# One stream of 2368 score slots in place of 1184 turns of two scores, with B's maxima packed in full banks and spread beside the next unit

## The chip, the core and the metric

The kernel runs on one core of a Trainium2 chip. Its five engines work side by side and meet by semaphores: TensorE (PE in the profile, its weight loads PEld), VectorE (DVE), ScalarE (ACT), GpSimd (POOL) and SyncE (SP), which issues most DMAs. Each engine takes its instructions in order. Matmul results land in PSUM, eight banks of 512 fp32 columns on 128 partitions, and have to be read from there by VectorE or ScalarE. The metric is the device time of one execution in microseconds (us).

## The reference

Two attention layers run over the same 2048 x 512 input with 32 heads of 16 dimensions. Their outputs are mixed by a gate per token.

```
A: p = softmax(q k^T / 4) over all 2048 keys; o = p v; a = o @ wo
B: four segments of 512 tokens; in each
   p = softmax(q k^T / 4 + causal mask) over the segment's own keys; a_dot = p v
   a_mem = phi(q) M / (phi(q) z + 1e-6)          phi(t) = t + 1 if t > 0, else exp(t)
   o = g * a_mem + (1 - g) * a_dot               g = sigmoid(beta), by head
   M += phi(k)^T v;  z += sum of phi(k)
   b = o @ wo
out = s * a + (1 - s) * b                        s = sigmoid(x . gate_w)
```

## The kernel before

**First stage.** The projections of both sides are made chunk by chunk of 512 tokens (`CH`), each as three products of a high and a low part (L312), and put in DRAM, q and k with both halves, v with a column of ones. B's memory is built on the way. Some maxima are computed here already (`some_max`).

**Main stage.** The work is cut in units: a side (A or B), a group `g` of four heads (eight groups) and a chunk `c` of 512 queries (four). That makes 32 units of A and 32 of B, one of each after the other.
In a unit of A, the scores of a block of 128 keys against the 512 queries are one matmul for each head, 128 keys on the partitions, 512 columns (st, L626). A head's q and k, cut in parts, take 50 rows, so heads 0 and 1 lie in the lower 64 partitions and heads 2 and 3 in the upper 64 (`rows`): two products on different halves can run at the same time. ScalarE takes the exponential of a bank (L638) into `p`. Value products (ops, L674) multiply `p` by v and the ones for the four heads side by side, 17 columns of weights each, and add up over all keys in one PSUM bank `ops`. At the end of a unit ScalarE copies `ops` (L678) and SP stores it (L679).

**Maxima.** The softmax subtracts each row's maximum before the exponential. For that, the scores are computed a second time the other way round, 128 queries on the partitions and 512 keys in the columns (sm, L180), and VectorE reduces each bank (L197). This runs `LEAD` turns ahead of the scores. When a unit's maxima are there, `finish_max` reduces them once more and negates them (L159), POOL splits them into a high and a low part (L163, L164), PE transposes them (L170), ScalarE copies them (L172), and two DMAs, issued on ScalarE's queue (L174), write them as two more rows of the q tile, rows 48 and 49. The unit's first score needs these rows.
For B, of the 4 x 4 blocks of 128 queries by 128 keys only the lower triangle counts. Before, a unit's maxima are five turns of two banks. The first two turns take query block 3 against all 512 keys with a mask added (L209). In the others a bank holds 256 columns that VectorE reduces straight (L217, L223) and 256 columns on the diagonal that ScalarE copies to `dg` (L216, L222), POOL masks (L225) and VectorE reduces `MASK_T` turns later.

**Order.** All is written by hand (`manual_schedule`); the loop over turns at the end of `gated_mix` sets it. A turn is two scores and two maxima, alternating, then the value products of the turn `LAG` = 4 before, then transposes (`run_late`), reduces that were put off (`after_max`), and output products. Everything else hangs on turn numbers: `beside` (loads, factors, scaling) and `fill` (output products, six at a time, four such runs for 128 rows of the output). A unit of A has 32 turns (8 x 4 head pairs by key blocks), one of B five. Heads 0 and 1 are scored in even turns while the maxima take 2 and 3; odd turns the other way round.
PSUM in the main stage: three banks for maxima (`sm_ps`), three for scores (`st_ps`), one for `ops`, one for output products and transposes (`ms_ps`).

**End of the pipeline.** When a chunk's units are done, the sums of the softmax are inverted (`recip`, `invert`), the outputs are scaled (POOL), split in two parts, and multiplied by both `wo` (`out_products`, 24 matmuls for 128 rows, L762). The last chunk is done in pieces (`piece`).

Of the kernel before, what the change touches and what calls it, by code (L numbers as in the profile page):

```python
# [19 lines left out]
D = 512  # L20
# [12 lines left out]
TURNS = {"A": 32, "B": 5}  # L33
LEAD = 44
LAG = 4
LATE_T = 6
MASK_T = 4
PRE = 10
NK = 10
# [3 lines left out]
def gated_mix(ctx, tc, x, xT, wqkv, a_wo, b_wq, b_wk, b_wv, b_wo, beta, gate_w, out):  # L43
# [8 lines left out]
    for side in "AB":  # L52
        for o in range(NO):
            for c in range(NCH):
# [17 lines left out]
    cmask = const.tile([128, CH], F32, name="cmask")  # L72
    nc.gpsimd.memset(cmask, 0.0)
    nc.gpsimd.affine_select(out=cmask, in_=cmask, pattern=[[-1, CH]], base=384, channel_multiplier=1,
                            compare_op=ALU.is_ge, fill=MASKED)
# [18 lines left out]
    sm_ps = ctx.enter_context(tc.tile_pool(name="sm_ps", bufs=3, space=PSUM))  # L94


    units = []
    for c in range(NCH):
        for g in range(NG):
            pair = [("A", g, c), ("B", g, c)]  # L100
            units += pair if c < NCH - 1 else pair[::-1]
    units.insert(1, units.pop(2))
    turns = [(u, j) for u in units for j in range(TURNS[u[0]])]
    first = {}
    for t, (u, j) in enumerate(turns):
        if j == 0:
            first[u] = t
    end = {u: first[u] + TURNS[u[0]] for u in units}
    seg_end = {(s, c): max(end[s, g, c] for g in range(NG)) for s in "AB" for c in range(NCH)}

# [7 lines left out]

    kbuf = [kp.tile([128, 2, CH], F32R, name=f"k{i}") for i in range(NK)]
    knext = [0]  # L120
# [11 lines left out]
    def load_k(u, kc):  # L132

        side, g, c = u
        t = kbuf[knext[0] % NK]
        knext[0] += 1
# [12 lines left out]
    pmt = {}  # L149
    late = []  # L150
    masked = []

    pmB = [mp.tile([128, 4, 4, 2], F32, name=f"pmB{i}", bufs=1) for i in range(2)]
# [3 lines left out]
    def finish_max(u):  # L157
        nm = mp.tile([128, 4, 4], F32, tag="nm", name="nm")
        nc.vector.tensor_reduce(nm, pmt.pop(u), axis=AX.X, op=ALU.max, negate=True)  # L159
# [7 lines left out]
    def transpose_max(u, ms, pool, tag):  # L167
# [5 lines left out]
        for r in range(2):  # L173
            nc.scalar.dma_start(raw(qt[u])[64 * r + 48:64 * r + 50], raw(mt)[16 * r:16 * r + 16])  # L174
# [4 lines left out]
    def max_product(ps, u, h, s, n0, n, k):  # L179
        nc.tensor.matmul(ps[:, n0:n0 + n], rows(qt[u][:, :, s * 128:(s + 1) * 128], h, 48), rows(k[:, :, :n], h, 48),  # L180
                         start=True, stop=True)

    def max_parts(m):

        u, j = turns[m]
        side, g, c = u
        if j == 0:
            pmt[u] = (mp.tile([128, 4, 4, 4], F32, tag="pmA", name="pm") if side == "A" else pmB[(c * NG + g) % 2])
        pm = pmt[u]
        heads = (2, 3) if m % 2 == 0 else (0, 1)  # L190

        def part_a(e):

            ps = sm_ps.tile([128, CH], F32, tag="sm", name="sm")
            h, s, kc = heads[e], j // 2 % 4, j // 8
            max_product(ps, u, h, s, 0, CH, kt_[u, kc])
            nc.vector.tensor_reduce(pm[:, h, s, kc:kc + 1], ps, axis=AX.X, op=ALU.max)  # L197

        dg = dp.tile([128, 4, 128], F32, tag="dg", name="dg") if side == "B" and j > 1 else None

        def part_b(e):
            k = kt_[u, c]
            ps = sm_ps.tile([128, CH], F32, tag="sm", name="sm")
            if j < 2:
                h = heads[e]
                max_product(ps, u, h, 3, 0, CH, k)
                nc.vector.tensor_tensor_reduce(ps, ps, cmask, 1.0, -3.0e38, ALU.add, ALU.max, pm[:, h, 3, 0:1])  # L209
                return  # L210
            two = dg[:, 2 * e:2 * e + 2]
            if j < 4:
                h = heads[e]
                max_product(ps, u, h, 0, 0, 128, k)
                max_product(ps, u, h, 2, 128, 384, k)
                nc.scalar.copy(two, blocked(ps)[:, 0::3])  # L216
                nc.vector.tensor_reduce(pm[:, h, 2, 0:1], ps[:, 128:384], axis=AX.X, op=ALU.max)  # L217
            else:
                h = heads[0] if e == 0 else 2 - heads[0]
                for f in range(2):  # L220
                    max_product(ps, u, h + f, 1, 256 * f, 256, k)
                nc.scalar.copy(two, blocked(ps)[:, 1::2])  # L222
                nc.vector.tensor_reduce(pm[:, h:h + 2, 1, 0], blocked(ps)[:, 0::2], axis=AX.X, op=ALU.max)  # L223
            if e == 1:
                nc.gpsimd.affine_select(out=dg, in_=dg, pattern=[[0, 4], [-1, 128]], base=0, channel_multiplier=1,  # L225
                                        compare_op=ALU.is_ge, fill=MASKED)
                h0 = heads[0]

                def reduce():
                    if j < 4:  # L230
                        out, src = pm[:, h0:h0 + 2, 0::2, 1], dg.rearrange("p (h s) t -> p h s t", h=2)
                        nc.vector.tensor_reduce(out, src, axis=AX.X, op=ALU.max)  # L232
                    else:
                        for h, two in ((h0, dg[:, 0:2]), (2 - h0, dg[:, 2:4])):
                            nc.vector.tensor_reduce(pm[:, h:h + 2, 1, 1], two, axis=AX.X, op=ALU.max)  # L235
# [751 lines left out]
```

## Time and profile before

| | |
|---|---|
| Three runs | 2124.81, 2143.61, 2156.91 us (median 2143.61) |
| The profiled execution's own time | 2130.38 us |
| Its span, first to last instruction | 2128.7 us |
| Mean granted clock of TensorE | 0.966 |
| PE busy | 2033.5 us (96%), 16705 matmuls |
| PEld busy | 950.7 us (45%) |
| DVE busy | 1645.0 us (77%) |
| ACT busy | 1510.5 us (71%) |
| POOL busy | 315.1 us (15%) |
| 345 to 2105 us alone | PE 1698.6, DVE 1456.9, ACT 1384.8, POOL 293.8 of 1760; clock 0.97, DMA share 0.35 |

How to read it: busy time is a union, so an engine whose instructions overlap by their tails counts each moment once. A matmul's row begins when it is issued and its end is modelled; PE counts as busy whenever a row is open, at half the clock too. So PE's 96% says that PE is rarely without a row, not that it streams all the time.

The costliest groups of the page, with the mean time of one in ns and the idle time before them:

```profile
L197 DVE TENSOR_REDUCE pm<-sm 128x1 f32<-128x512 f32 x2048 | 1270.7, 683 | 162.3 <-PE sm L180 133.5
L638 ACT ACTIVATE p<-st 128x512 f32<-128x512 f32 x2048 | 1134.7, 604 | 310.1 <-PE sm L180 163.2
L180 PE MATMUL sm<-k,qA 48*128 48x512 f32 x2048 | 804.0, 467 | 10.5 <-DVE pm L197 8.3
L626 PE MATMUL st<-qA,k 50*128 50x512 f32 x2048 | 772.7, 455 | 20.6 <-ACT p L638 19.3
L674 PE MATMUL ops<-p,vA 128*17 128x256 f32 x8192 | 659.8, 395 | 12.6 <-ACT oraw L678 12.5
```

Each value product of the program stands twice in the trace, as two passes.

### The profile page before, as it was taken

The numbers are of one execution on the slowest core, as the hardware profiler recorded it, in microseconds if no ns is written. First come the engines' busy times: TensorE is split into PE (matmuls) and PEld (weight loads), VectorE is DVE, ScalarE is ACT, GpSimd is POOL, SyncE is SP. The second block draws the span as 40 slices with busy tenths as digits, with TensorE's granted clock in tenths as the row PEclk, the third lists the DMA queues.
The fourth block names the chain that finished last, engine by engine and source line by source line (L and its number), as shares of the span: only waits on it lengthen the run. The fifth ranks groups of instructions, "written<-read, shape, count | busy, mean of one in ns | idle before, by whom it ended". The sixth has DMA issues, their size and how long they took to land.

```text
span 2128.7 us, 43282 instructions
## 1 busy us (share of the span) xinstructions
PE 2033.5 (96%) x16705; PEld 950.7 (45%) x16705; DVE 1645.0 (77%) x2996; ACT 1510.5 (71%) x2945; POOL 315.1 (15%) x512
## 2 busy tenths in 40 slices
PE   7999999999999999999999999999999999999996
PEld 6887664343333333444443333444433434343343
DVE  3235896899988988788889998878889998877810
ACT  3234335788887877787778887778788887776773
POOL 3000001132100102111100032111011231101130
PEclk9999998999999999899999998999999999998998
DMA  6667545545522235332222362222232642322311
GB/s 199 222 212 252 174 150 171 144 107 146 145 77 77 77 100 137 77 82 74 70 67 78 93 164 79 73 77 63 81 84 81 162 102 73 82 80 70 104 52 36
DMA packets 113629, 233.81 MB, mean 110 GB/s; under 512 B 23840, under 2 KB 38208, under 8 KB 111760
## 3 DMA queue, kind: packets, MB, share of 16 engines
q1 hardware_dynamic: 109600, 228.48, 37.9%
q8 instruction: 133, 2.18, 0.4%
q10 hardware_dynamic: 2592, 1.57, 0.3%
q0 software_dynamic: 1232, 0.99, 0.2%
q14 instruction: 72, 0.59, 0.1%
HBM read 159.07 MB, written 70.66 MB: 108 GB/s over the span
## 4 chain that ended last, share of the span: by engine, by line
PE 80%; DVE 10%; ACT 6%; DMA 2%; issue 2%; ACTq 1%; SPq 0%; DVEq 0%
PE st L626 31%; PE ops L674 27%; PE pr L312 11%; DVE pm L197 6%; PE sm L180 4%; PE fin L762 4%; ACT p L638 3%; PE fin L893 1%; DVE pmB L232 1%; DVE pmB L235 1%; ACT oraw L678 1%; ACT dg L216 1%; ACTq L174 1%; PE num L468 1%; PE mt_ps L170 0%
## 5 line engine op out<-in xcount | busy, mean ns | idle before, releaser
L197 DVE TENSOR_REDUCE pm<-sm 128x1 f32<-128x512 f32 x2048 | 1270.7, 683 | 162.3 <-PE sm L180 133.5
L638 ACT ACTIVATE p<-st 128x512 f32<-128x512 f32 x2048 | 1134.7, 604 | 310.1 <-PE sm L180 163.2
L180 PE MATMUL sm<-k,qA 48*128 48x512 f32 x2048 | 804.0, 467 | 10.5 <-DVE pm L197 8.3
L626 PE MATMUL st<-qA,k 50*128 50x512 f32 x2048 | 772.7, 455 | 20.6 <-ACT p L638 19.3
L674 PE MATMUL ops<-p,vA 128*17 128x256 f32 x8192 | 659.8, 395 | 12.6 <-ACT oraw L678 12.5
L626 PEld LDWEIGHTS st<-qA,k 50*128 50x128 f32 x2048 | 311.9, 189 | 464.4 <-ACT p L638 379.9
L180 PEld LDWEIGHTS sm<-k,qA 48*128 48x128 f32 x2048 | 325.5, 189 | 45.9 <-DVE pm L197 26.3
L674 PEld LDWEIGHTS ops<-p,vA 128*17 128x17 f32 x8192 | 136.9, 96 | 346.8 <-issue 318.0
L163 POOL CAST ms<-nm 128x16 fp32r<-128x16 f32 x64 | 12.7, 199 | 1038.6 <-DVE nm L159 1038.5
L645 ACT ACTIVATE p<-st 128x512 f32<-128x512 f32 x256 | 141.2, 604 | 22.0 <-PE sm L180 13.0
L626 PE MATMUL st<-qB,k 50*128 50x384 f32 (+3 forms) x512 | 133.5, 364 | 18.7 <-ACT p L638 17.2
L180 PE MATMUL sm<-k,qB 48*128 48x128 f32 (+3 forms) x512 | 144.7, 368 | 1.3 <-DVE pmB L217 1.2
L626 PEld LDWEIGHTS st<-qB,k 50*128 50x128 f32 x512 | 77.5, 195 | 99.7 <-ACT p L645 51.5
L360 DVE TENSOR_TENSOR q<-pr,q 128x512 fp32r<-128x512 f32 x64 | 44.0, 687 | 96.3 <-ACT q L353 90.0
L353 ACT CAST q<-pr 128x512 fp32r<-128x512 f32 x64 | 37.5, 586 | 95.8 <-PE pr L312 68.2
L674 PE MATMUL ops<-p,vB 128*17 128x256 f32 (+1 forms) x1536 | 103.7, 358 | 0.0
L630 POOL TENSOR_SCALAR_AFFINE_SELECT p<-p 128x512 f32<-128x512 f32 x128 | 79.6, 635 | 162.2 <-ACT p L645 137.3
L217 DVE TENSOR_REDUCE pmB<-sm 128x1 f32<-128x256 f32 x128 | 54.4, 425 | 53.1 <-ACT dg L216 52.9
L180 PEld LDWEIGHTS sm<-k,qB 48*128 48x128 f32 x512 | 77.9, 184 | 20.7 <-DVE pmB L217 15.8
L209 DVE CUSTOM_DVE_ANT_0 sm<-sm,cmask 128x512 f32<-128x512 f32 x128 | 84.4, 718 | 2.5 <-PE sm L180 2.5
L225 POOL TENSOR_SCALAR_AFFINE_SELECT dg<-dg 128x512 f32<-128x512 f32 x96 | 60.9, 635 | 157.4 <-ACT dg L216 133.5
L312 PE MATMUL pr<-xh,wql 128*128 128x512 f32 x128 | 55.1, 430 | 6.1 <-ACT xh L404 6.1
(171 smaller groups left out, 1667.8 us busy)
## 6 DMA issues: line engine op xcount, KB each, us to landing
k<-kdA SPq DMA_DIRECT2D x256, 128.0 KB
vA<-vdA SPq DMA_DIRECT2D x32, 544.0 KB
k<-kdA SPq DMA_DIRECT2D x256, 64.0 KB
qdA<-q SPq DMA_DIRECT2D x32, 256.0 KB
kdA<-q SPq DMA_DIRECT2D x32, 256.0 KB
qdB<-q SPq DMA_DIRECT2D x32, 256.0 KB
qA<-qdA SPq DMA_DIRECT2D x64, 128.0 KB
kdB<-q SPq DMA_DIRECT2D x32, 256.0 KB
```

The lines of the kernel that those rows point to most:

```text
L180: nc.tensor.matmul(ps[:, n0:n0 + n], rows(qt[u][:, :, s * 128:(s + 1) * 128], h, 48), rows(k[:, :, :n], h, 48), start=True, stop=True)
L197: nc.vector.tensor_reduce(pm[:, h, s, kc:kc + 1], ps, axis=AX.X, op=ALU.max)
L209: nc.vector.tensor_tensor_reduce(ps, ps, cmask, 1.0, -3.0e38, ALU.add, ALU.max, pm[:, h, 3, 0:1])
L217: nc.vector.tensor_reduce(pm[:, h, 2, 0:1], ps[:, 128:384], axis=AX.X, op=ALU.max)
L225: nc.gpsimd.affine_select(out=dg, in_=dg, pattern=[[0, 4], [-1, 128]], base=0, channel_multiplier=1, compare_op=ALU.is_ge, fill=MASKED)
L312: nc.tensor.matmul(ps, l(a, k), r(b, k), start=(n == 0), stop=(n == 11))
L626: nc.tensor.matmul(ps[:, n0:n0 + CH - q0], rows(k[:, :, b * 128:(b + 1) * 128], h, 50), rows(q[:, :, q0:], h, 50), start=True, stop=True)
L630: nc.gpsimd.affine_select(out=x, in_=x, pattern=[[0, 4], [1, 128]], base=0, channel_multiplier=-1, compare_op=ALU.is_ge, fill=0.0)
L638: nc.scalar.activation(p[:, h], ps, AF.Exp, scale=SCALE)
L645: nc.scalar.activation(p[:, h], ps, AF.Exp, scale=SCALE)
L674: nc.tensor.matmul(ops[32 * h:32 * h + 17, q0:q0 + w], v[n][:, 17 * h:17 * h + 17], p[:, h, c0:c0 + w], start=(j == 0), stop=(j == TURNS[s ...
L762: nc.tensor.matmul(ps, l[:, o], r[:, o], start=(n == 0), stop=(n == 23))
```

## The change

The main stage's turn of two scores becomes a slot of one: one score bank and one bank of maxima, 64 slots for a unit of A and ten for one of B, 2368 in all. The maxima have a list of their own (`maxs`), as long as the slots and 96 slots ahead. In it B's ten banks stand seven places apart among the maxima of the next unit of A. B's banks are packed full: in each row half two of diagonal blocks alone (four 128 x 128 products, copied to `dg` and masked as before), two with one block of query block 1 and three of query block 3, and one with query block 2 of two heads. The mask that was added (`cmask`) goes.
Heads are scored in the order 0, 2, 1, 3, so that score and maximum swap row halves at each slot.
Values wait until a block of keys has all its four heads, and go after each third slot (`BURST`), as wide as the queue allows: 512 columns for A. Output products run in three runs of eight in place of a burst of values, each run in a score bank, copied out and added by POOL. Transposes take score banks too. `sm_ps` has four banks, `ms_ps` is gone. The maxima's rows of q are written by DMAs on SP's queue instead of ScalarE's. A has eight k buffers and B two, where ten were shared. Numbers of turns become numbers of slots throughout, and some loads and stores of 1 MB are cut in four.

```diff
-TURNS = {"A": 32, "B": 5}
-LEAD = 44
-LAG = 4
-LATE_T = 6
-MASK_T = 4
-PRE = 10
-NK = 10
+SLOTS = {"A": 64, "B": 10}
+NU = 32
+LEAD = 96
+BURST = 3
+RUN = 8
+GAP = {"A": 3, "B": 5}
+MASK_T = 8
+LATE_T = 8
+PRE = 20
+NKA, NKB = 8, 2
...
+    maxs = []
+    for k in range(NU):
+        mine = {u: iter(range(32)) for u in range(2)}
+        bs = [k - 1] if 0 < k < NU - 1 else [k - 1, k] if k else []
+        start, apart = (34, 3) if k == 1 else (6, 7) if k < NU - 1 else (24, 3)
+        theirs = {r: [(unit("B", b), (r, i)) for b in bs for i in range(5)] for r in range(2)}
+        for p in range(64 + 10 * len(bs)):
+            r = (len(maxs) + 1) % 2
+            i = (p - start) // apart
+            if (p - start) % apart == 0 and 0 <= i < 10 * len(bs):
+                maxs.append(theirs[r].pop(0))
+            else:
+                maxs.append((unit("A", k), (r, next(mine[r]))))
...
-            nc.scalar.dma_start(raw(qt[u])[64 * r + 48:64 * r + 50], raw(mt)[16 * r:16 * r + 16])
+            nc.sync.dma_start(raw(qt[u])[64 * r + 48:64 * r + 50], raw(mt)[16 * r:16 * r + 16])
...
+            if i < 2:
+                for n in range(4):
+                    b = i + 2 * (n % 2)
+                    max_product(ps, u, h0 + n // 2, b, 128 * n, 128, k, 128 * b)
+                dg = dp.tile([128, 4, 128], F32, tag="dg", name="dg")
+                nc.scalar.copy(dg, blocked(ps))
...
+                todo.append((m + MASK_T, lambda: nc.vector.tensor_reduce(
+                    to, dg.rearrange("p (h s) t -> p h s t", h=2), axis=AX.X, op=ALU.max)))
+            elif i < 4:
+                h = h0 + i - 2
+                max_product(ps, u, h, 1, 0, 128, k)
+                max_product(ps, u, h, 3, 128, 384, k)
+                nc.vector.tensor_reduce(pm[:, 1, h, 3:7], blocked(ps), axis=AX.X, op=ALU.max)
+            else:
+                for f in range(2):
+                    max_product(ps, u, h0 + f, 2, 256 * f, 256, k)
...
+        if m == last_max[u]:
+            def finish():
+                late.append((m + MASK_T + 2 + LATE_T, u, finish_max(u)))
+            todo.append((m + (MASK_T + 1 if side == "B" else 0), finish))
...
-    ms_ps = ctx.enter_context(tc.tile_pool(name="ms_ps", bufs=1, space=PSUM, reuse_waits="tile"))
+    sm_ps = ctx.enter_context(tc.tile_pool(name="sm_ps", bufs=4, space=PSUM, reuse_waits="tile"))
...
+        h = (0, 2, 1, 3)[j % 4]
...
+            queue.extend((n + GAP[side], u, i) for i in range(j // 4 * 4, j + 1))
...
+            for h in range(4):
+                nc.tensor.matmul(ops[32 * h:32 * h + 17, q0:q0 + 128 * w], v[:, 17 * h:17 * h + 17], p[:, h, c0:c0 + 128 * w],
+                                 start=(i == 0), stop=done, tile_position=(0, 32 * h))
...
+    def out_products(c, b, i):
+
+        ps = st_ps.tile([128, D], F32, tag="st", name="fin")
+        for n in range(RUN * i, RUN * i + RUN):
...
+        t = fr.tile([128, D], F32, tag="res" if i == 0 else "more", name="res", bufs=2 if i == 0 else 1)
+        nc.scalar.copy(t, ps)
...
+        nc.gpsimd.tensor_add(t0, t0, t)
...
+    while n < nS or queue or waiting or beside or fill:
+        for f in beside.pop(n, []):
             f()
+        waiting += fill.pop(n, [])
+        if n < nS:
+            score_part(n)
+        m = n + LEAD
+        if m < nS:
             loads(m + PRE)
+            max_part(m, sm_ps)
+        run_todo(m)
+        if n % BURST == BURST - 1 or n >= nS:
+
+            filled[0] = bool(waiting) and not filled[0] and m < nS
+            if not filled[0]:
+                some_values(n)
+
+                run_late(st_ps, "st", m + 1)
+            if waiting and (filled[0] or m >= nS):
+                waiting.pop(0)()
+        n += 1
```

More of the change, by code (lines that the diff above doesn't have):

```diff
@@ L149, in gated_mix @@
     pmt = {}
+    todo = []
     late = []
-    masked = []
-    pmB = [mp.tile([128, 4, 4, 2], F32, name=f"pmB{i}", bufs=1) for i in range(2)]
+    pmB = [mp.tile([128, 2, 4, 8], F32, name=f"pmB{i}", bufs=1) for i in range(2)]
     for t in pmB:
@@ L196, in part_a @@
             max_product(ps, u, h, s, 0, CH, kt_[u, kc])
             nc.vector.tensor_reduce(pm[:, h, s, kc:kc + 1], ps, axis=AX.X, op=ALU.max)
-        dg = dp.tile([128, 4, 128], F32, tag="dg", name="dg") if side == "B" and j > 1 else None
-        def part_b(e):
+        else:
             k = kt_[u, c]
[L205 to L224, printed above, removed]
@@ L229, in reduce @@
[L229 to L235, printed above, removed]
-                masked.append((m + MASK_T, reduce))
@@ L609, in gated_mix, with score_part, score @@
     pt_ = {}
[L611 to L613 removed]
+    queue = []
+    def score_part(n):
+        u, j = slots[n]
         side, g, c = u
         q = qt[u]
[L616 to L625 removed]
+        if j % 4 == 0:
+            pt_[u, j // 4] = pp.tile([128, 4, CH], F32, tag="p", name="p")
+        p = pt_[u, j // 4]
+        h = (0, 2, 1, 3)[j % 4]
+        def score(ps, h, b, k, n0, q0):
             nc.tensor.matmul(ps[:, n0:n0 + CH - q0], rows(k[:, :, b * 128:(b + 1) * 128], h, 50),
@@ L832, in gated_mix @@
     c = NCH - 1
-    nT = len(turns)
     fins = {}
```

381 lines of the change are left out of this document (168 added, 213 removed).

## The prediction

> **What bounds the kernel now.** I read the clock first (mean 0.966), then the chain of waits, whose shares by engine are
>
> ```profile
> PE 80%; DVE 10%; ACT 6%; DMA 2%; issue 2%; ACTq 1%; SPq 0%; DVEq 0%
> ```
>
> so PE mostly. Next the timeline of one undisturbed A turn, because a share is a mean over unlike parts:
>
> ```profile
> 1002.00 0.50 PE L626 MATMUL st<-qA,k 50*128 50x512 f32 x1
> 1002.00 0.50 PE L180 MATMUL sm<-k,qA 48*128 48x512 f32 x1
> 1002.33 0.39 PE L626 MATMUL st<-qA,k 50*128 50x512 f32 x1
> 1002.34 0.39 PE L180 MATMUL sm<-k,qA 48*128 48x512 f32 x1
> 1002.66 0.63 PE L674 MATMUL ops<-p,vA 128*17 128x256 f32 x8
> 1003.22 0.50 PE L626 MATMUL st<-qA,k 50*128 50x512 f32 x1
> ```
>
> A score (st) and a maximum (sm) start together: they use opposite halves of the array's rows. From pair to pair 0.33 us, then eight value products, and 0.88 us from the second pair to the next turn's first: 1.22 us a turn. Near 2072 us, where no maxima are left, turns still come 1.22 apart (value rows at 2072.07, 2073.28, 2074.50), so this is PE's own pace and not VectorE's. The other two engines, where work is queued for them:
>
> ```profile
> 1040.86 3.67 DVE L197 TENSOR_REDUCE pm<-sm 128x1 f32<-128x512 f32 x6
> ```
>
> ```profile
> 343.87 3.54 ACT L638 ACTIVATE p<-st 128x512 f32<-128x512 f32 x7
> ```
>
> One lasts 0.68 and 0.60 us, so one follows another after (3.67-0.68)/5 = 0.598 us on VectorE and (3.54-0.60)/6 = 0.49 on ScalarE. A turn needs 1.20 of VectorE and 0.98 of ScalarE: VectorE is just under PE.
>
> Then the stops between turns. B's maxima, cut into 256 columns:
>
> ```profile
> 1029.48 0.42 DVE L217 TENSOR_REDUCE pmB<-sm 128x1 f32<-128x256 f32 x1 [0.34 <-ACT dg L216]
> 1030.24 0.42 DVE L217 TENSOR_REDUCE pmB<-sm 128x1 f32<-128x256 f32 x1 [0.34 <-ACT dg L216]
> ```
>
> VectorE and ScalarE take turns on one bank, 0.77 us a reduce. Six output products:
>
> ```profile
> 1008.09 0.73 PE L762 MATMUL fin<-wolA,hA 128*128 128x512 f32 x2
> 1008.66 1.09 PE L762 MATMUL fin<-wohA,hA 128*128 128x512 f32 x4
> 1009.68 0.49 PE L626 MATMUL st<-qA,k 50*128 50x512 f32 x1
> ```
>
> 0.23 us each in the run of four; VectorE's next reduce, at 1010.25, follows 1.51 us of idleness. The maxima's way back into q, issued on ScalarE's queue, and the clock around it (busy time of PE, its loads, VectorE, ScalarE and POOL; then clock and DMA):
>
> ```profile
> 609.34 1.28 ACTq L174 DMA_DIRECT2D qB<-mt  x2
> 610.66 1.09 ACT L638 ACTIVATE p<-st 128x512 f32<-128x512 f32 x2 [1.36 <-PE sm L180]
> ```
>
> ```profile
> 608.90:612.40 3.50, 2.36 (x21) 0.93 (x24) 2.88 (x5) 2.14 (x6) 0.00 (x0) 1.00 0.02 5
> 612.40:619.20 6.80, 6.80 (x44) 1.96 (x38) 3.64 (x7) 3.91 (x8) 0.00 (x0) 0.50 0.77 207
> ```
>
> ScalarE issues for 1.28 us and computes nothing, PE's score at 611.31 waits 0.68 us for it, and after a window with PE 67% busy the clock (0.50) is halved for 6.8 us. Value rows start 2.13 us apart there instead of 1.22: 2.9 us lost.
>
> **The sum before.** First score at 340.4, last copy of ops at 2105, span 2128.7. Between copies (L678) an A unit without output products takes 42.5 us and a B unit 7.9: 32 x 50.4 = 1613. Forty-eight stops of 1.5: 72. The stage's mean clock, 0.97, is about 110 us at half speed, 43% of it lost: 48. That leaves some 32 of the measured 1765 for the last unit and the factors. The profiled execution took 2130.4, the median of the three runs is 2143.6.
>
> **The change, part by part.**
>
> Values. A block of 128 keys now waits for four slots and goes as four heads of 512 columns (2048 products by the program's order instead of 4096 of 256). The second pass of 256 columns starts 0.21 us after the first in the trace, so 512 add 0.21 to each of two passes: the way round values goes from 0.88 to 1.30 us, but once for four slots instead of twice. Pairs that follow each other without values have no undisturbed row here: I bound their pitch by 0.23 (output products) and 0.33, and take 0.33 for the first, which reloads after the switch, and 0.23 for the others. Four slots: 1.30 + 0.33 + 2 x 0.23 = 2.10, or 2.3 with 0.33 throughout; two turns now take 2.43. An A unit: 33.6 us of PE (to 37) instead of 39.
>
> VectorE then sets the pace. A pair of units has 74 slots and one full bank of maxima each: 74 x 0.598 = 44.3, and two last reduces (L159) of about 0.2 extra: 44.7. This holds B's too: ten reduces of 0.60 instead of masked ones (0.65 apart, L209), halves of 0.77 and five of dg; the 0.34 us alternation goes, since a bank is read by one engine only.
>
> ScalarE: 74 exponentials and 4 full-bank copies to dg at 0.49, two copies of ops at 0.59, two of mt at 0.25: 40 us. It loses 2 x 1.28 us of issuing.
>
> PE for B: ten pairs in pieces (about 3 us), sixteen 128-column maxima and the split ones (some 2.4), four value groups with switches (2.9), two transposes (1.1): 9.4, bounded by 7.5 and 11. PE 43 (41 to 48), VectorE 44.7, ScalarE 40 a pair. Three engines this close don't overlap perfectly; four sm banks hold 4 x 0.598 = 2.4 us of VectorE's work, more than the 1.30 of a value burst plus 0.56 until the next result, so I add only 1.3: **46 us a pair**, against 50.4.
>
> Output products: 36 runs of eight instead of 48 of six, each in place of a value burst, from a score bank. 8 x 0.23 + 0.3 = 2.15 of PE, of which PE's slack (1.7 a pair, 2.2 runs a pair) hides about a third: 1.5 each, 54 us; 2.15 if there is no slack. Their 24 more copies (0.59) and POOL's 24 additions (1.28) lie beside; ScalarE has 5 us a pair, POOL is 15% busy.
>
> POOL's 32 more selects of dg (0.64) have MASK_T, eight slots or 4.9 us, before VectorE's reduce stands in its queue behind them; were POOL late, all later maxima would wait, about a microsecond each time. B's values wait five slots for POOL's select of p, 3 us for exponential, 0.64 to 1.27 and semaphores: at the edge, in the 1.3.
>
> The maxima's way back moves to SP's queue, behind q, k and v loads (0.42 us an issue) and output stores; SP issues some 40 a pair, 17 of 46 us. Behind each mt transfer wait k loads for maxima 20 slots later and the store of ops: nothing near. But the schedule shrinks its margin for B: by the program's order 6 to 8 scores lie between B's transpose and B's first score, which needs it (29 turns before); A keeps 16 to 20. 6 to 8 slots are 3.7 to 4.9 us. In them fit the transpose (0.4), ScalarE's queue (up to 1), the copy (0.25), two issues (0.8) and the landing: 1.5 us by the packets of L174's transfers in the trace, 3.8 by the row of k<-ones, also 8 KB. So 3.9 to 6.3 us, a stop of 0 to 2.6; nearer the first row, which is the same transfer: 0.4 a unit, 13 us (0 to 80). SP's transfers are taken in ring order on each DMA engine, behind its own loads, says the Trainium skill (DMA: Bandwidth & Descriptors, Queues, rings and completion order), while ScalarE's had a ring to themselves. By that, q's 8 KB would wait for a v load of 544 KB where one stands before it, some 2 us at the highest 252 GB/s of the profile: nearer 60 us than 13. The main stage's DMA share of 0.35 says that mostly nothing stands there.
>
> The clock: the idle windows that halved it came with the issues on ScalarE; B's new stop could do the same. I take 25 us (0 to 48). SP's extra 4-way split loads and stores, cmask, buffer sets (8 A, 2 B): 0.
>
> Sum: 343 (8 more maxima ahead) + 1472 + 19 (36 reciprocals of 0.34, nine products) + 54 + 25 (last unit) + 25 (clock) + 13 + 24 (tail) = 1975 span. With 2 around it and the few us by which the median stood above the profile: **1980**.
>
> **Rivals.** (1) PE stays the bound: pitch 0.33 throughout, 48.5 a pair, products 2.15, clock 48: 343 + 1552 + 77 + 25 + 48 + 13 + 24 = 2082. For it: PE is busy 9 of 10 everywhere. Against: half of the switches go. Chance 0.13.
> (2) The pairing is lost, and it ends slower. Before, halves alternate within a turn; now score and maximum swap each slot (lower, upper, upper, lower), so a score follows a maximum on the same half. If it then waits the maximum out, each slot pays 0.23 more: 43 + 17 = 60 a pair, about 2430. It decides from half of the slots on. Against: at 344.52, 345.01 and 345.50, first turns without values, pairs with that swap between them still start as pairs. 0.07.
> (3) B's first score waits for q: each us costs 32. At 2.6 us, 2050; slower than now only from 5.5 us. 0.08.
> (4) The clock: PE, waiting shortly for VectorE at each bank, is throttled more. One 6.8 us stretch a pair costs 32 x 2.9 = 93 instead of 25: 2048; two a pair: 2140. Against: windows at the A turn's rhythm, with its drains, stay at 1.00. The Trainium skill (TensorE: Matmul & The Clock Gate, A second HAM failure mode) describes such short idling between groups as cause of an oscillating clock. 0.07.
>
> **How the numbers follow.** Forecast 0.65. Low end: VectorE's floor, 343 + 1430 + 19 + 36 + 15 + 24, near 1870. High end: rival 1, 2080. 2% is 43 us, a little more than the 32 between the three runs. Faster by over 2% (under 2101): forecast, most of 1, 3 and 4: 0.87. Within: 0.06. Slower: 0.07, mostly rival 2.
>
> **What would show it.** Reduces 0.60 apart in A units; a pair near 46 us between copies; value rows of 512 once in four slots; st and sm starting together, 0.23 apart; no 1.28 us of issue on ScalarE; few halved stretches. Wrong if B's first score shows a wait for qB<-mt over 1 us, if PE never waits for VectorE, or if st and sm start apart.

## The result, and the profile after

The changed kernel takes 2022.54 us, median of four runs (2016.17 to 2026.5); the kernel before 2150.26 (2124.81 to 2157.03). The ratio is 0.9474, 95% interval 0.939 to 0.9558. The forecast was 1980 in a range of 1870 to 2080: the direction and the range held, and the time came out 42 us above the number. The profiled execution took 2020.8 us, its span is 2019.1, its mean clock 0.98. Ratios here and below leave out the runs of a slower state, so they are not the quotients of the medians.

First the page of the changed kernel: the chain's shares by engine, and the groups that answer to those of before.

```profile
PE 81%; ACT 11%; DVE 4%; DMA 2%; issue 2%; POOL 0%; SPq 0%; ACTq 0%; DVEq 0%; POOLq 0%
...
L219 DVE TENSOR_REDUCE pm<-sm 128x1 f32<-128x512 f32 x2048 | 1289.8, 682 | 156.8 <-PE sm L204 132.4
L642 ACT ACTIVATE p<-st 128x512 f32<-128x512 f32 x2304 | 1214.9, 609 | 211.7 <-PE sm L204 162.2
L619 PE MATMUL st<-qA,kA 50*128 50x512 f32 x2048 | 762.2, 454 | 36.2 <-ACT p L642 31.3
L204 PE MATMUL sm<-kA,qA 48*128 48x512 f32 x2048 | 785.0, 456 | 1.8 <-DVE pmB L240 0.8
...
L675 PE MATMUL ops<-p,vA 128*17 128x512 f32 x4096 | 544.6, 607 | 0.0
```

VectorE's share of the chain fell from 10% to 4% and ScalarE's rose from 6% to 11%. If VectorE set the pace, as forecast, the maxima (sm, L204) would wait for its reduces; they wait 1.8 us in all. It is the scores (st, L619) that wait, 36.2 us, 31.3 of them for ScalarE's exponential. The value products went from 659.8 us to 544.6.

The timeline of PE in an undisturbed unit of A, where before a turn of two scores and a value block of 256 took 1.22 us:

```profile
601.33 0.50 PE L619 MATMUL st<-qA,kA 50*128 50x512 f32 x1
601.34 0.73 PE L204 MATMUL sm<-kA,qA 48*128 48x512 f32 x2
601.67 0.62 PE L619 MATMUL st<-qA,kA 50*128 50x512 f32 x2
601.91 0.39 PE L204 MATMUL sm<-kA,qA 48*128 48x512 f32 x1
602.51 0.50 PE L619 MATMUL st<-qA,kA 50*128 50x512 f32 x1 [0.22 <-ACT p L642]
...
603.00 0.50 PE L619 MATMUL st<-qA,kA 50*128 50x512 f32 x1
...
603.49 0.50 PE L619 MATMUL st<-qA,kA 50*128 50x512 f32 x1
...
603.98 1.05 PE L675 MATMUL ops<-p,vA 128*17 128x512 f32 x8
604.96 0.50 PE L619 MATMUL st<-qA,kA 50*128 50x512 f32 x1
```

Values are due after every third slot, but a block is ready only after every fourth, so one turn in four finds none, and six slots follow each other. The first three scores come 0.34 and 0.23 us apart; the fourth waits, and the fourth to sixth come 0.49 apart, which is the pitch of ScalarE's exponentials: the three score banks are full. The six slots and their block take 604.96 - 601.33 = 3.63 us. The next turn, with its block, starts at 604.96 and ends at 606.84: 1.88. Twelve slots take 3.63 + 2 x 1.88 = 7.39, where VectorE would need 12 x 0.598 = 7.18.

Where the time came from, by the two profiled executions: a pair of units without output products and without a halved clock, between 540 and 840 us, fell from 50.4 (two pairs) to 47.5 (six pairs, 46.6 to 48.1; copies of `ops` of A), and the time at half clock between the first and the last store of A's `ops` from 99 us to 48. A fit of the pairs' times on their halved time and their output products gives 0.67 us lost for each halved us after the change. This is a high figure: a clock at half speed alone can lose at most 0.5, so the fit counts stops that go with the stretches too; without the last two pairs it gives 0.52, and in the kernel before 0.40. What is worked out with 0.67 below is an upper estimate.

Three windows of the changed kernel, the last in a halved stretch (the columns are the ends, the length, busy time of PE, its loads, VectorE, ScalarE and POOL, then clock, DMA share and GB/s):

```profile
1141.20:1144.60 3.40, 3.18 (x21) 1.10 (x17) 3.24 (x6) 3.17 (x7) 1.27 (x2) 1.00 0.03 7
1144.60:1148.00 3.40, 2.89 (x28) 1.81 (x28) 3.30 (x6) 3.15 (x7) 1.17 (x2) 1.00 0.21 77
1148.00:1151.40 3.40, 3.40 (x19) 1.09 (x15) 2.25 (x5) 1.75 (x4) 1.28 (x3) 0.50 0.46 135
```

In the middle window PE is busy 85%: six slots of a unit of B with no values among them, and a wait of 0.48 us for an exponential. The next 3.4 us run at half the clock. Before the change nine of the twelve such stretches between the first and the last store of A's `ops` lasted 6.8 us or more; here ten of twelve last 3.4.

### The profile page after: what moved, and what is told of

Read it like the earlier page. It is cut to its first block, busy times and chain, and to the rows that moved or that the text cites. A ratio compares the mean times of both kernels' runs of the same rounds, so it can differ in the third digit from the quotient of the medians.

```text
span 2019.1 us, 34830 instructions
## 1 busy us (share of the span) xinstructions
PE 1929.0 (96%) x12481; PEld 928.8 (46%) x12481; DVE 1614.2 (80%) x2740; ACT 1485.6 (74%) x2905; POOL 364.0 (18%) x566
## 4 chain that ended last, share of the span: by engine, by line
PE 81%; ACT 11%; DVE 4%; DMA 2%; issue 2%; POOL 0%; SPq 0%; ACTq 0%; DVEq 0%; POOLq 0%
PE ops L675 27%; PE st L619 26%; PE pr L311 12%; PE sm L204 9%; ACT p L642 8%; PE fin L758 4%; DVE pm L219 2%; PE fin L890 1%; ACT dg L230 1%; PE num L467 1%; ACT oraw L679 1%; PE mt_ps L194 1%; PE mps L498 0%; DMA qdA<-q 0%; DMA qdB<-q 0%
## 5 line engine op out<-in xcount | busy, mean ns | idle before, releaser
L619 PE MATMUL st<-qA,kA 50*128 50x512 f32 x2048 | 762.2, 454 | 36.2 <-ACT p L642 31.3
L204 PE MATMUL sm<-kA,qA 48*128 48x512 f32 x2048 | 785.0, 456 | 1.8 <-DVE pmB L240 0.8
L619 PEld LDWEIGHTS st<-qA,kA 50*128 50x128 f32 x2048 | 345.4, 188 | 597.7 <-ACT p L642 509.4
L675 PE MATMUL ops<-p,vA 128*17 128x512 f32 x4096 | 544.6, 607 | 0.0
L204 PEld LDWEIGHTS sm<-kA,qA 48*128 48x128 f32 x2048 | 343.9, 187 | 25.2 <-DVE pm L219 12.5
L204 PE MATMUL sm<-kB,qB 48*128 48x128 f32 (+2 forms) x896 | 176.2, 301 | 0.0
L204 PEld LDWEIGHTS sm<-kB,qB 48*128 48x128 f32 x896 | 138.4, 193 | 7.9 <-DVE pm L219 1.2
L619 PE MATMUL st<-qB,kB 50*128 50x384 f32 (+3 forms) x512 | 127.8, 348 | 12.6 <-ACT p L642 10.9
L619 PEld LDWEIGHTS st<-qB,kB 50*128 50x128 f32 x512 | 73.9, 186 | 96.7 <-ACT p L642 81.0
L240 DVE TENSOR_REDUCE pmB<-sm 128x4 f32<-128x512 f32 x128 | 87.0, 680 | 5.3 <-PE sm L204 5.1
L675 PE MATMUL ops<-p,vB 128*17 128x512 f32 (+3 forms) x1024 | 89.5, 453 | 0.1
```

Source lines behind the costliest of these rows:

```text
L240: nc.vector.tensor_reduce(pm[:, 1, h, 3:7], blocked(ps), axis=AX.X, op=ALU.max)
L619: nc.tensor.matmul(ps[:, n0:n0 + CH - q0], rows(k[:, :, b * 128:(b + 1) * 128], h, 50), rows(q[:, :, q0:], h, 50), start=True, stop=True)
L675: nc.tensor.matmul(ops[32 * h:32 * h + 17, q0:q0 + 128 * w], v[:, 17 * h:17 * h + 17], p[:, h, c0:c0 + 128 * w], start=(i == 0), stop=done ...
```

## The experiments

The theory that the forecast stands for: VectorE sets the pace (46 us a pair by the forecast), because wider value blocks and full maxima banks took PE below it. Its rivals: PE still binds; the moved DMA issue made most of the gain; halves, late rows of q, or the clock. Times below are medians of four runs where nothing else is said, ratios are to the kernel before in the same session. Pairs and halved time are taken as above from each trace.

| | us | ratio (95%) | undisturbed pair | halved us |
|---|---|---|---|---|
| before (profiled span 2128.7) | 2150.26 | 1 | 50.4 | 99 |
| changed (2019.1) | 2022.54 | 0.9474 (0.939 to 0.9558) | 47.5 | 48 |
| x1 issue back on ScalarE (2095.1) | 2110.84 | 0.9854 (0.9787 to 0.9921) | 49.4 | 97 |
| x2 before, issue on SP (2054.0) | 2062.21 | 0.9661 (0.9585 to 0.9737) | 49.4 | 10 |
| x3 values of 256 (2000.9) | 2001.07 | 0.9356 (0.9298 to 0.9413) | 47.7 | 0 |
| x4 half reduces (1997.5) | 2000.21 | 0.9361 (0.9299 to 0.9422) | 47.3 | 31 |
| x5 one product a run (1982.5) | 1983.83 | 0.9223 (0.9156 to 0.9291) | 47.5 | 68 |
| x8 transpose 4 slots later (2078.4) | 2073.78 | 0.9642 (0.9569 to 0.9715) | 47.5 | 119 |
| x9 same half in a slot (2122.9) | 2153.73 (ten runs) | 0.9993 (0.9923 to 1.0062) | 51.3 | 51 |
| x10 B's maxima close (2044.1) | 2050.62 | 0.9553 (0.9463 to 0.9644) | 47.9 | 75 |
| y1 four score banks (2099.5) | 2099.73 | 0.9829 (0.9747 to 0.9912) | 50.5 | 108 |
| y2 the same, turns of four (2176.4) | 2178.89 | 1.0206 (1.0135 to 1.0276) | 53.0 | 106 |
| x7 turns of four (2089.4) | 2101.45 | 0.9829 (0.9756 to 0.9903) | 49.7 | 44 |
| y5 values of three slots (1974.2) | 1973.84 (six runs) | 0.9189 (0.9144 to 0.9233) | 46.7 | 10 |

**Is VectorE the pace?** x4 halves the width of A's reduces.

```diff
-            nc.vector.tensor_reduce(pm[:, h, s, kc:kc + 1], ps, axis=AX.X, op=ALU.max)
+            nc.vector.tensor_reduce(pm[:, h, s, kc:kc + 1], ps[:, :256], axis=AX.X, op=ALU.max)
```

> The changed kernel with A's 2048 VectorE reduces reading 256 of the 512 columns of each bank; half of the keys are left out of A's maxima. PE's and ScalarE's work stays. Theory (VectorE sets the pace of the changed kernel): a reduce takes 0.4 us or less instead of 0.6, and a pair of units falls from 47.3 to PE's own 43 to 45: 70 to 140 us faster, 1880 to 1950. Rival (PE's pace still binds, VectorE is just behind it): within 20 us of 2022.

2000.21: 22 us less, just outside the rival's 20 and far from 70. From its page, the reduce, and from its timeline, the run of six slots:

```profile
L219 DVE TENSOR_REDUCE pm<-sm 128x1 f32<-128x256 f32 x2048 | 783.3, 418 | 577.9 <-PE sm L204 479.0
```

```profile
591.93 0.50 PE L619 MATMUL st<-qA,kA 50*128 50x512 f32 x1
...
593.11 0.50 PE L619 MATMUL st<-qA,kA 50*128 50x512 f32 x1 [0.22 <-ACT p L642]
...
594.58 1.05 PE L675 MATMUL ops<-p,vA 128*17 128x512 f32 x8
595.56 0.50 PE L619 MATMUL st<-qA,kA 50*128 50x512 f32 x1
```

VectorE lost 506 us of work and gained 421 of idleness before these reduces; the six slots still take 595.56 - 591.93 = 3.63 us with the same wait of 0.22, and the pair 47.3 instead of 47.5. So VectorE is not what sets the pace in the changed kernel. Of the 22 us at most 17 x 0.67 = 11 go with the clock, and 32 x 0.2 = 6 are the pairs.

**What did the moved issue make?** x1 undoes it in the changed kernel (below); x2 makes the same edit the other way in the kernel before, and nothing else.

```diff
-            nc.sync.dma_start(raw(qt[u])[64 * r + 48:64 * r + 50], raw(mt)[16 * r:16 * r + 16])
+            nc.scalar.dma_start(raw(qt[u])[64 * r + 48:64 * r + 50], raw(mt)[16 * r:16 * r + 16])
```

> The changed kernel with the two transfers that bring the maxima back into q issued on ScalarE's queue again, as before the change. Theory (the changed kernel goes at VectorE's pace, ScalarE has about 5 us a pair of units to spare): the two issues of 1.28 us per pair come back; the exponentials behind them are late by that, PE's next score waits about 0.7 us, and perhaps a halved clock stretch follows: between 0 and 1.4 us a pair, so 2022 to 2067 us, with rows of 1.28 us on ScalarE's queue at the transfer. Rival (most of the gain came from the moved issue, not from the wider blocks): 60 to 80 us slower, 2085 to 2105.

> The kernel before with one edit: the maxima's transfers into q issued on SP's queue instead of ScalarE's. Theory (that issue was one cause among several: 64 stops of about 0.7 to 1.3 us and part of the 16 halved stretches): 45 to 80 us faster than before, about 2070 to 2100, with fewer halved stretches; a pair without output products stays near 50 us. Rival A (the issue is the whole of the change's gain): 2020 to 2035. Rival B (the stop on ScalarE was beside the path and the halved stretches come from something else): no difference beyond 10 us, and as many halved stretches.

x1 takes 2110.84, the rival's case and a little beyond; x2 2062.21, 8 us below the theory's range for it but above that of rival A. A piece of x1's timeline (ScalarE, ScalarE's queue, PE):

```profile
640.11 3.04 ACT L642 ACTIVATE p<-st 128x512 f32<-128x512 f32 x6 [1.38 <-DMA qB<-mt]
...
640.76 0.50 PE L619 MATMUL st<-qA,kA 50*128 50x512 f32 x1 [0.45 <-ACT p L642]
...
643.27 1.28 ACTq L198 DMA_DIRECT2D qA<-mt  x2
...
643.86 1.91 PE L675 MATMUL ops<-p,vA 128*17 128x512 f32 x8
644.60 0.60 ACT L642 ACTIVATE p<-st 128x512 f32<-128x512 f32 x1 [1.36 <-PE st L619]
```

Each pair of issues stops ScalarE for 1.3 us; the score behind it waits 0.45, and three full score banks leave nothing else to do. At 643.86 eight value products take 1.91 us instead of 1.05: the clock has halved, behind 3.4 us in which the scores wait for banks and come 0.49 apart. An undisturbed pair is 1.9 us longer, 61 us over 32 pairs, and the halved time doubles. In the kernel before, the same one line is worth about 75 us between profiled executions: 1.0 us a pair, and 89 us less at half clock. So this line makes the larger part of the gain. How much of its share comes by way of the clock differs: the pairs leave some 43 of 75 us for it and all else in the kernel before (75 - 32), and some 15 of 76 in the changed one (76 - 61).

**What did the wide blocks make?** x3 puts values back to 256 columns after every two slots.

```diff
-BURST = 3
+BURST = 2
...
-            while (queue and most and queue[0][0] <= n and queue[0][1] == u and (i + w) // 4 == i // 4
+            while (w < 2 and queue and most and queue[0][0] <= n and queue[0][1] == u and (i + w) // 4 == i // 4
...
-                some_values(n)
+                ready = sum(e[0] <= n for e in queue)
+                some_values(n, 2 if ready <= 4 else 4)
```

> The changed kernel with its values going in two passes of 256 columns after every two slots, as before the change, instead of 512 columns after four; all else stays. Theory (the wider block took about 0.35 us from every four slots of PE, and thereby made VectorE the one that sets the pace): PE needs 2.43 us for four slots again against VectorE's 2.39; a pair of units goes from 47.3 to 48.5 to 50, and the output products find no slack of PE: 2060 to 2130 us. Rival (PE has slack either way, the gain came from the queue and from B's maxima): within 10 us of the changed kernel.

2001.07, some 21 us faster than the changed kernel, so neither case. All four of its runs (1995.75 to 2009.08) lie below all four of the changed kernel, though these are of another session and the two intervals of the ratio overlap a little. Its timeline of PE:

```profile
607.61 0.50 PE L619 MATMUL st<-qA,kA 50*128 50x512 f32 x1
...
608.27 0.63 PE L675 MATMUL ops<-p,vA 128*17 128x256 f32 x8
608.83 0.50 PE L619 MATMUL st<-qA,kA 50*128 50x512 f32 x1
```

1.22 us for two slots, just the turn of before, without a wait: twelve slots take 7.3, against 7.39 for the wide blocks. What these save in products they lose in the run of six. And the clock is not halved once between the first and the last store of A's `ops` (48 us in the changed kernel, worth at most 0.67 x 48 = 32). That is not for want of waits: in most pairs a score of B still waits some 0.75 us for an exponential in x3, 20.8 us in 29 times between 405 and 1900 us. So the packed stream, with all that came with it, and the queue make the gain, and the wide blocks, as they are queued, seem to take some of it back. The parts of the packed stream were not taken apart.

**The score banks.** The theory now: PE is held by score banks wherever more than three slots follow each other without values, and the clock halves after such waits (for this second part see the last section). x7 makes every turn four slots long; y1 moves a bank from the maxima to the scores (the last unit's fourth bank of outputs, which was one of theirs, moves with it); y2 does both.

```diff
-BURST = 3
+BURST = 4
```

```diff
+    st4_ps = ctx.enter_context(tc.tile_pool(name="st4_ps", bufs=1, space=PSUM, reuse_waits="tile"))
-    sm_ps = ctx.enter_context(tc.tile_pool(name="sm_ps", bufs=4, space=PSUM, reuse_waits="tile"))
+    sm_ps = ctx.enter_context(tc.tile_pool(name="sm_ps", bufs=3, space=PSUM, reuse_waits="tile"))
...
-        ps = st_ps.tile([128, CH], F32, tag="st", name="st")
+        fourth = n % 4 == 3 and n < nS - 92
+        ps = (st4_ps if fourth else st_ps).tile([128, CH], F32, tag="st", name="st")
...
```

> The changed kernel with its values' turn after every four slots instead of three, and the banks as they are (three for scores, four for maxima). Theory (the score banks bind): the fourth score of each turn waits for the first exponential, 0.5 to 0.6 us after its result, in every turn instead of in one of three: 2.4 to 2.6 us a turn, 47 to 51 us a pair, 2010 to 2100. Rival (score banks don't matter, VectorE's pace binds): 46 to 47.5 a pair, 1990 to 2022.

> The changed kernel with one bank moved from the maxima to the scores (four score banks, every fourth score in the new one; three banks for maxima). Theory now (in the changed kernel PE runs out of score banks: where six slots follow each other without a value burst, the fourth to sixth score wait for ScalarE's exponentials and come 0.49 us apart instead of 0.33, about 0.2 to 0.7 us in every twelve slots; the halved clock stretches go with these waits): a pair of units falls from 47.3 to 45 to 46.5, 20 to 70 us faster than 2022, 1955 to 2000. Rival A (VectorE's pace or its order of banks binds as soon as it has three banks only): 47 to 50 a pair, 2020 to 2100. Rival B (ScalarE's own busy time binds): no difference beyond 10 us.

> The changed kernel with four score banks and three for the maxima, and its values' turn after every four slots instead of three, so that each turn has four scores, four maxima and one value block. Theory (the score banks bind): four slots and a block fit without a wait, 2.1 us by the forecast's rows, so that VectorE's 0.598 a slot sets the pace: 44.5 to 46 a pair, 1930 to 1990. Rival (a steady wait of PE for VectorE in each turn keeps the clock halved more often, or three maxima banks run empty in the longer turn): 2020 or more.

x7 came nearly as the theory had it: 2101.45, just above its 2010 to 2100, with 48.7 and 50.7 us a pair in turn. But its halved time, 44 us, is no more than the changed kernel's, though it waits more than twice as long for score banks. The waits of PE say where (us in all, times, the longest); x7 first, then the changed kernel:

```profile
PE st L619 <- ACT p L642: 90.4, 359, 1.2
```

```profile
PE st L619 <- ACT p L642: 42.2, 139, 1.2
```

y1 and y2 missed by 100 us and more, and went as their rivals said that name the maxima's three banks. The timeline of y1, six slots:

```profile
653.36 0.50 PE L204 MATMUL sm<-kA,qA 48*128 48x512 f32 x1
...
653.98 0.50 PE L204 MATMUL sm<-kA,qA 48*128 48x512 f32 x1
...
654.58 0.49 PE L204 MATMUL sm<-kA,qA 48*128 48x512 f32 x1
```

The maxima now come 0.62 and 0.60 us apart, VectorE's pace, and each holds up the score behind it in PE's order, so that pairs no longer start together. Both consumers lie so close to PE that each needs its banks: in this arrangement a fourth bank is worth more to the maxima than to the scores. That leaves the order of the work as a way to take the wait away.

**Does it go without the run of six?** y5 keeps the turn of three slots and the banks, and takes three slots' values, 384 columns, in each.

```diff
-                some_values(n)
+                ready = sum(e[0] <= n for e in queue)
+                some_values(n, 8 if n >= nS else 3 if ready <= 6 else 6)
```

> The changed kernel with its values' turn, after every three slots as now, taking 384 columns (three slots) instead of all that is ready, so that no run of six slots goes without values. Theory (what holds the changed kernel back is the run of six slots, in which PE waits for score banks, and the clock that halves after such waits): by the rows of 256 and 512 columns a turn takes PE some 1.75 us and VectorE 1.79, so a pair of units comes near 45.5 to 47, the waits of scores for exponentials fall below 15 us in all, and there are fewer than five halved stretches before the last unit: 1950 to 1990, below the narrow version's 2001. Rival (blocks cut in two cost PE what the waits cost, or the clock halves all the same): 2000 to 2040.

1973.84 (1969.02 to 1978.46), the fastest of all and inside the theory's range. Its waits and its timeline:

```profile
PE st L619 <- ACT p L642: 6.4, 21, 1.2
```

```profile
600.86 0.49 PE L619 MATMUL st<-qA,kA 50*128 50x512 f32 x1
...
601.75 0.84 PE L675 MATMUL ops<-p,vA 128*17 128x128 f32 x16
602.53 0.50 PE L619 MATMUL st<-qA,kA 50*128 50x512 f32 x1
```

These turns are 1.67, 1.69 and 1.73 us long (600.86, 602.53, 604.22, 605.95), though every block is cut in two (3 and 1, 2 and 2, 1 and 3 of its columns' quarters). That is PE's own pace, faster than VectorE's 3 x 0.598 = 1.79, and it lasts only until VectorE is behind. Further on in the same unit ScalarE's three exponentials of each turn, which wait for PE, come at VectorE's pace:

```profile
610.05 1.57 ACT L642 ACTIVATE p<-st 128x512 f32<-128x512 f32 x3 [0.23 <-PE sm L204]
611.85 1.57 ACT L642 ACTIVATE p<-st 128x512 f32<-128x512 f32 x3 [0.22 <-PE sm L204]
613.64 1.57 ACT L642 ACTIVATE p<-st 128x512 f32<-128x512 f32 x3 [0.22 <-PE sm L204]
```

They are 1.80 and 1.79 us apart, and a turn's third maximum starts (610.11) only when a reduce has ended (610.06). From 540 to 840 us VectorE is busy 291.39 of 300 us (289.76 in the changed kernel). So by the trace, without a test, VectorE sets the pace in this part of the unit once the run of six is gone, as the forecast had it; little more is to be had without taking work from VectorE too. The waits for score banks fell from 42.2 us to 6.4, the halved time from 48 to 10, all of it in the last two pairs. Only how values are shared out among the turns was changed, and it is worth 45 us between the profiled executions: so much the uneven turns had cost, 32 x 0.8 = 26 of it in the pairs and the rest mostly with the clock.

**The output products.** x5 makes one matmul of each run of eight.

> The changed kernel with one matmul instead of eight in each run of output products; seven eighths of the output products of the chunks before the last are left out, copies, additions and stores stay. By the forecast's term (36 runs at 1.5 us) it is about 45 us faster, 1977. By the fit of the pairs' times on their number of product matmuls in the changed kernel's trace (0.26 us a matmul, 252 fewer) it is 65 us faster, 1957. If the runs cost their full 2.15 us and their side effects too, up to 75 us.

1983.83, 39 us faster, at 20 us more of halved time: 39 + 0.67 x 20 = 52 at most without that, between the forecast's term and the fit. So 7 of 8 matmuls cost 39 to 52 us over 36 runs, 1.1 to 1.45 each run, which leaves the fit of 0.26 us a matmul too high: part of what it found belongs to the run, not to its matmuls. In x5 the undisturbed pairs that still hold two or three such runs (50.0, 49.8, 51.0, 47.4, 47.7, 49.8) take 49.3 on the mean, 1.8 more than those without, 0.8 a run. That can be its bank, its copy, its one matmul and the turn of values that it displaces; these were not told apart. Together about 2 us a run.

**B's rows of q.** x8 puts the transposes four slots later.

```diff
-LATE_T = 8
+LATE_T = 12
```

> The changed kernel with the maxima's transpose put four slots later (12 instead of 8), so that B's first score comes 2 to 4 slots behind B's transpose instead of 6 to 8. Theory (the way back through the transpose, the copy, the issue on SP and the landing takes 3 to 4 us, which 6 to 8 slots of 0.6 us just hide): a stop of 1 to 2.4 us appears before B's first score in each of the 32 pairs, 30 to 80 us slower, and the length of the stop gives the length of the way. Rival (the way is shorter than 2 us): no difference beyond 10 us.

2073.78, 51 us slower. A wait that the changed kernel hasn't got, in x8's waits:

```profile
PE st L619 <- DMA qB<-mt: 31.1, 26, 4.4
```

The mean, 1.2 us, hides two kinds. Thirteen of the 26 waits last 1.6 to 4.4 us, and during each, or within 3 us of its end, a stretch at half clock begins; here is one, and the two windows around its end:

```profile
637.40 0.66 PE L619 MATMUL st<-qB,kB 50*128 50x512 f32 x1 [1.64 <-DMA qB<-mt]
```

```profile
634.10:637.50 3.40, 1.58 (x12) 0.94 (x11) 3.15 (x6) 2.79 (x7) 0.63 (x1) 1.00 0.02 5
637.50:640.90 3.40, 3.40 (x16) 1.12 (x18) 0.69 (x1) 0.85 (x2) 0.00 (x0) 0.50 0.00 0
```

The other thirteen last 0.6 us or less, and the undisturbed pairs, which have only such, take 47.5 us as in the changed kernel. So most of the loss comes by the long stops and the halved time, which rose from 48 to 119. The score of 637.40 starts 3.02 us after B's transpose (634.38), one held for the other half's rows 3.39 after it (684.10 and 687.49). Outside the last unit the changed kernel leaves 4.5 us at the least, so B's rows come with little more than 1 us to spare.

**The halves.** x9 turns the heads' order round.

```diff
-        h = (0, 2, 1, 3)[j % 4]
+        h = (2, 0, 3, 1)[j % 4]
```

> The changed kernel with the halves' order of the scores turned round (heads 2, 0, 3, 1 instead of 0, 2, 1, 3), so that score and maximum of one slot use the same half of the array's rows. Theory (they run at the same time only on opposite halves; the second rival of the forecast took 0.23 us more a slot): a pair of units near 60 us, 2350 to 2450 in all, with st and sm starting 0.23 us or more apart. Rival (two products on one half follow each other at the pace of two on opposite halves): no difference beyond 20 us.

2153.73: the whole gain is gone, but 200 us less than expected are lost. Score and maximum of a slot no longer start together in x9's timeline:

```profile
622.47 0.50 PE L619 MATMUL st<-qA,kA 50*128 50x512 f32 x1
622.81 0.40 PE L204 MATMUL sm<-kA,qA 48*128 48x512 f32 x1
622.96 0.50 PE L619 MATMUL st<-qA,kA 50*128 50x512 f32 x1
```

The maximum starts 0.34 us after the score; but a slot is still 0.49 us, as in the run of six of the changed kernel. The loss lies in the turns of three:

```profile
625.10 0.50 PE L619 MATMUL st<-qA,kA 50*128 50x512 f32 x2
...
627.23 0.51 PE L619 MATMUL st<-qA,kA 50*128 50x512 f32 x2
```

This one takes 2.13 us, where the changed kernel took 1.88. A pair takes 51.3, 3.8 more, not 14: the next slot's score, on the other half, starts 0.15 us behind the maximum and runs beside it.

**The spread.** x10 puts B's ten maxima three places apart instead of seven.

```diff
-        start, apart = (34, 3) if k == 1 else (6, 7) if k < NU - 1 else (24, 3)
+        start, apart = (34, 3) if k == 1 else (6, 3) if k < NU - 1 else (24, 3)
```

> The changed kernel with B's ten maxima put three places apart among A's instead of seven (places 6 to 33 instead of 6 to 69 of the 74 of each unit pair). Theory (each is one full bank and one reduce like A's, and only the dg way of GpSimd's select needs distance): 0 to 2 us a pair, 2022 to 2085, with waits for dg where the four masked banks follow each other. Rival 1 (the spread itself is worth as much as the pitch of VectorE: POOL's select and VectorE's second reduce pile up): over 70 us slower. Rival 2 (the maxima's rows come late for B in the changed kernel): earlier maxima make it faster by 10 us or more.

2050.62, 28 us slower, inside the theory's 0 to 63: 0.4 us more a pair (13 us), and 27 us more of halved time (18 at most). Earlier maxima made nothing faster, so rival 2 is out.

## Why the prediction was right, and where it was wrong

**The sum.** By the trace the main stage begins at 342 us, the last copy of `ops` is at 1996, and 23 us follow. 342 + 32 x 47.5 (1520) + 72 (products) + 32 (clock) + 30 (last unit and reciprocals, found as what is left, so no run shows it) + 23 = 2019. The forecast had 343 + 1472 + 54 + 25 + 44 + 13 + 24 = 1975.

**The pair, 46.** Right to 1.5 us for a reason that was wrong: "VectorE then sets the pace". The failing step is the one behind it: "four sm banks hold 4 x 0.598 = 2.4 us of VectorE's work ... so I add only 1.3". It counted the maxima's banks against a value burst and not the three score banks against six slots without one. The forecast had a row of this: the pairs without values that it cites at 344.52, 345.01 and 345.50 come 0.49 us apart, ScalarE's pitch, and it read from them only that score and maximum start together. The product counts of PE were right (a turn of three with its block takes 1.88), and VectorE's 7.18 for twelve slots is only 0.2 below the 7.39 that came out, so the wrong bound gave nearly the right number, by luck. The forecast named its own sign, "if PE never waits for VectorE", and that came true. So did "reduces 0.60 apart": where two engines are this close, a pace says little of what sets it, and it took x4 to tell. With even turns (y5) VectorE does set the pace for part of a unit, at 46.7 a pair, near the 46 that the forecast has for it.

**Values.** "Once for four slots instead of twice" was so, but it brought nothing: x3, with the old width, has pairs of 47.7 against 47.5 and no halvings. Evenly shared out (y5) wider blocks have pairs of 46.7. The forecast took the burst's place as regular; the queue's rule (ready every four slots, due every three) made it uneven.

**The maxima's way back.** The forecast saw each piece (1.28 us of issue, 0.68 of PE's wait, a window at half clock behind it), but gave the whole no term of its own; in its sum it vanished into VectorE's pace and, for a part, into a clock term of 25 instead of 48. x1 and x2 put it at some 75 us of the 110 between the profiled executions. Its danger, the late rows for B, was priced at 13 (0 to 80) and cost nothing: the way took 3.02 and 3.39 us in two stops of x8, where the forecast had 3.9 to 6.3. x8 also shows that nothing and 51 us lie four slots apart.

**Output products, 54.** About 2 us a run instead of 1.5: 72. PE had no slack to hide a third of a run in, since it, and not VectorE, was behind.

**Clock, 25.** At most 32: right in size. Rival 4 named short waits of PE for VectorE's banks; in the changed kernel they are waits for ScalarE's. Each of its twelve halved stretches begins within 2 us behind the end of a wait of a score of 0.3 to 1.2 us, most of them of 0.5, and none behind one of 0.2 us alone, like that at 602.51. But there are 48 such longer waits, so most bring no stretch, and what decides it stays open. The Trainium skill (TensorE: Matmul & The Clock Gate, A second HAM failure mode) describes short idling between matmul groups that cycle through PSUM banks as a cause of a clock that goes up and down. The changed kernel (42.2 us of waits for score banks, 48 halved) and y5 (6.4 and 10) agree; x3 (22.0 and 0) and x7 (90.4 and 44) show that the sum of such waits does not set the halved time.

**Rival 1** (PE stays the bound, 48.5 a pair) was nearer to the mechanism than the forecast, though not by its cause: y5 shows that switches at 0.33 were not the limit. (Its sum leaves out the 19 us for reciprocals that the forecast's has; with them it is 2101.) **Rival 2** was real and overpriced: x9 costs 3.8 a pair where 14 was said, because the forecast added the wait to each slot and forgot that the next slot overlaps it.

## What to carry to other kernels

When engines run within a few per cent of each other, count the banks between each producer and consumer against the longest run of work without a break, not the mean; an uneven order (due every three, ready every four) makes that run twice as long. A DMA issue on an engine that releases banks cost three things here: its issue time, the wait behind it, and in some pairs a stretch of half clock; price it as one term. Before calling an engine the bound, take work away from it.

## What was not expected of the hardware

The clock made much of the differences here: by the table, halved time runs from 0 to 119 us in kernels whose undisturbed pairs differ by 0.2 (x3 and x8). PE's busy time alone does not tell when it halves: in the changed kernel a window of 3.18 us busy of 3.4 had none behind it and one of 2.89 had, while in x1 one of 3.07 (640.50 to 643.90), its scores 0.49 apart, had one too. In x3 more than twenty windows with PE busy 2.5 to 2.7 of 3.4 us had none (2.65 from 500.9 to 504.3). Nor does it hang on the score banks alone: in y1, with 4.3 us of waits for these in all, most of its 108 halved us follow waits of maxima, 0.45 us and longer, for banks that VectorE reduces. A stop of 1.6 us was followed by half a clock all thirteen times (x8). Cutting a value block in two cost little: sixteen product rows of 128 and 256 columns stand for 0.84 us, as the eight of 384.
